# Top-k attention and a SoLU block on one core: from priorities to a fixed order of four engines

## The chip, the cores and the metric

The kernel runs on one core of a Trainium2 chip. The core has five engines that run side by side and meet through semaphores: PE (TensorE, matrix products and transposes; PEld is its weight load), ACT (ScalarE), DVE (VectorE), POOL (GpSimd) and SP (SyncE, which here issues the DMAs). Each takes its instructions in the order in which they stand in its program. The metric is device time in microseconds (us), less is better. Before the change it is 1582.19 us, the median of three runs (1580.61 to 1582.75).

## The reference

For each of 8 batches and 8 heads there are 576 queries, keys and values of 64 elements, in float32.

```
scores = q @ k.T / 8                              # 576 x 576 per head
kth    = the 32nd largest score of each row
P      = softmax(scores where scores >= kth, else -1e9)
attn   = P @ v                                    # 576 x 64 per head
x      = attn as 4608 tokens x 512                # the 8 heads side by side
h      = x @ w_in                                 # 512 -> 1024
solu   = h * softmax(h)
ln     = (solu - mean) / sqrt(var + 1e-6) * g_ln  # over the 1024
out    = ln @ w_out                               # 1024 -> 512
```

The weights arrive as float64, so the kernel first turns their words into float32 on DVE and POOL.

## The kernel before

**Work.** `fast_path` handles two heads of a batch at a time: 32 pairs. The 576 rows of two heads are 9 row tiles of 128 (four per head, and the two tails of 64 together). A general path follows in the program for inputs on which the search below fails; it is not taken here.

**One pair, in order of its data.** `load_qk` (SP) loads q and k. `prep_t`, `prep_m` (PE) transpose them, `prep_tc`, `prep_mc` (ACT) copy them out of PSUM. `moments` (PE) multiplies k with itself, `moments_c` (ACT) copies the result, `spread` (PE) multiplies it with q, `spread_v` and `spread_r` (DVE) reduce that to a spread per row, `first_p` (POOL, a power) and `first` (DVE) make a first threshold `t0` of it. `scores` (PE) makes the rows, `evac` (ACT) copies each row tile to SBUF as X. `count0` (DVE, `junkv`, L760) counts the scores over `t0`, nine instructions; `second` (DVE, its last at L775) makes `t1`; `count1` (ACT, `junka`, L783) counts again, nine instructions; `third` (DVE, L792 to L800) makes `t2`; `count2` (ACT, `sg`, L815) counts a third time. `side`, `nearest` (DVE, `al` L824 and `w` L836, L840) take the eight scores next to `t2`, `kth` (DVE) picks the 32nd. `exps` (ACT, E, L847), `keep` (DVE, L877), `inverse` (DVE) and `norm` (POOL, L892) make P; `transpose_p`, `transpose_last` (PE) and `copy_p`, `copy_last` (ACT) turn it; `attn_v` (PE) multiplies it with v, and `copy_v` (ACT, `xTm`, `xTt`) leaves x.

**One token tile.** 128 tokens, 36 in all: four per batch, and one of tails per two batches. `mm1` (PE, `h_ps`, L976), `hmax` (DVE), `hexp` (ACT), `solu` (DVE), `square` (ACT), `ln` (POOL, L1016 to L1021), `transpose_ln` (PE), `copy_ln` (ACT), `mm2` (PE, `o_ps`, L1040), `store` (ACT, then a DMA). A batch has four pairs, so a tile goes with each pair, and every eighth pair has one more.

**What sets the order.** Every step is put into a list with a time (`at`), the list is sorted, and the steps are traced in that order. The times are formulas, `STEP` = 38 apart from pair to pair, a token tile's from its own number. That trace is only a priority. Behind it a scheduler with a cost model of its own orders the instructions of each engine, and may take a later one first.

**Buffers.** PSUM has three pools of two buffers each: `ps_big` (two banks each: scores, `h_ps`, `y_ps`), `ps_tp` (one bank: all transposes and, before, `moments`) and `ps_o` (one bank: `om`, `ot`, `o_ps` and `y_t`). qm and km have one buffer each, X six, E three, `w_raw` two.

**Weights.** `load_w` (SP) loads a chunk of 128 x 512 float64, 16 chunks; `weights_step` runs a part of its conversion. Before, the first step of a chunk also issues the load of the next one.

Of the kernel before, what the change touches and what calls it, by code (L numbers as in the profile page):

```python
# [15 lines left out]
P = 128  # L16
# [427 lines left out]
def fast_path(  # L444
# [129 lines left out]
    xs = {}  # L574

# [27 lines left out]

    def prep_t(i):

        d = st[i]
        d["qkT"] = p2.tile([P, 2, S], F32, tag="qkT", name="qkT")
        tp = d["tp_t"] = ps_tp.tile([P, NM, P], F32, tag="tp", name="tp_t")
        for n, nm in enumerate("qk"):
            nc.tensor.transpose(  # L610
                tp[:, 0, n * ST : (n + 1) * ST], d[nm + "t"].rearrange("p h d -> p (h d)"),
                ident[0:ST, 0:ST],
            )

# [39 lines left out]
    def moments_c(i):  # L654
        d = st[i]
        nc.scalar.copy(out=d["mom"][:, 0:D], in_=d["tm"][:, 0:D])

    def spread(i):
# [4 lines left out]
        d["yt"] = ps_o.tile([P, 512], F32, tag="o", name="y_t")[:, 0 : D + 1]  # L663
# [93 lines left out]
    def count0(i, j):  # L757
# [4 lines left out]
            op0=ALU.is_ge, op1=ALU.add, accum_out=d["c0"][:, j : j + 1],  # L762
        )

    def second(i):
# [11 lines left out]
        d["n1"] = small.tile([P, NT], F32, tag="n1", name="n1")  # L777
        d["n2"] = small.tile([P, NT], F32, tag="n2", name="n2")

    def count1(i, j):  # L780
# [4 lines left out]
            bias=d["t1"][:, j : j + 1], accum_out=d["n1"][:, j : j + 1],  # L785
        )

    def third(i):
# [16 lines left out]
        d["al"] = small.tile([P, NT], F32, tag="al", name="al")  # L805
        d["w8"] = small.tile([P, NT, 8], F32, tag="w8", name="w8")
# [5 lines left out]
    def count2(i, j):  # L812
# [4 lines left out]
            bias=d["t2"][:, j : j + 1], accum_out=d["n2"][:, j : j + 1],  # L817
        )

    def side(i, g):  # L820
# [4 lines left out]
            out=d["al"][:, js], in0=d["n2"][:, js], scalar=512.5, in1=d["tt"][:, js],  # L825
# [3 lines left out]
    def nearest(i, j):  # L829
# [10 lines left out]
        nc.vector.max(d["w8"][:, j, :], w)  # L840

    def exps(i, g):
        d = st[i]
        if g == 0:
            d["E"] = [None] * NG
        d["E"][g] = p3.tile([P, 3, S], F32, tag="E", name="E")
        nc.scalar.activation(out=d["E"][g], in_=d["X"][g], func=AF.Exp)  # L847

    def kth(i):
# [13 lines left out]
        nc.vector.tensor_tensor(out=hot, in0=hot, in1=d["w8"], op=ALU.mult)  # L863
# [8 lines left out]
        d["rden"] = small.tile([P, NT], F32, tag="rden", name="rden")  # L872
# [24 lines left out]
    def p_of(i, j):  # L897
        return st[i]["E"][j // 3][:, j % 3, :]
# [5 lines left out]

    def copy_p(i, j):
        d = st[i]
        if j == 0:
            d["PT"] = [None, None]
        if j % 4 == 0 and j < 2 * NM:
            d["PT"][j // 4] = p2.tile([P, 2, NM + 1, 2 * P], F32, tag="PT", name="PT")  # L910
        if j < 2 * NM:
            t, h = divmod(j, 2)
            dst = d["PT"][t // 2][:, h, 0:NM, t % 2 * P : (t % 2 + 1) * P]
        else:
            d["PTt"] = p1.tile([P, NM + 1, P], F32, tag="PTt", name="PTt")
            dst = d["PTt"][:, 0:NM, :]
# [8 lines left out]
    def copy_last(i, part):  # L925
        d = st[i]
        tp = d.pop(("tpl", part))
        if part == 2:
            nc.scalar.copy(out=d["PTt"][0:ST, NM, :], in_=tp[0:ST, 0, :])
            return  # L930
        dst = d["PT"][part][0:ST, :, NM, :].rearrange("p h (t s) -> p t h s", t=2)
        nc.scalar.copy(out=dst, in_=tp[0:ST].rearrange("p (t h) s -> p t h s", h=2))

    def attn_v(i, part):
        b, hp = pairs[i]
        d = st[i]
        if part == 0:
            if hp == 0:
                xs["m", b] = p2.tile([P, NP, SM], F32, tag="xTm", name="xTm")
                if b % 2 == 0:  # L940
                    xs["t", b // 2] = p2.tile([P, NP, 2 * ST], F32, tag="xTt", name="xTt")
            d["om"] = ps_o.tile([P, 512], F32, tag="o", name="om")
        elif part == 2:
            d["ot"] = ps_o.tile([P, 512], F32, tag="o", name="ot")
        vm, vt = d["v"]
        o = d["ot"][:, 0:ST] if part == 2 else d["om"][:, part * 2 * P : (part + 1) * 2 * P]

        for c in range(NM + 1):
# [22 lines left out]
    def mm1(d):  # L971
        x = d["x"]()
        h = ps_big.tile([P, 2, 512], F32, tag="big", name="h_ps")
        for half in range(2):
            for c in range(NP):
                nc.tensor.matmul(  # L976
                    out=h[:, half, :], lhsT=x[:, c, :],
                    rhs=w_in[:, c, half * 512 : (half + 1) * 512],
                    start=(c == 0), stop=(c == NP - 1),
                )  # L980
        d["h"] = h.rearrange("p a f -> p (a f)")

    def hmax(d):
        d["nmax"] = small.tile([P, 1], F32, tag="hmax", name="hmax")
        nc.vector.tensor_reduce(out=d["nmax"], in_=d["h"], axis=AX.X, op=ALU.max, negate=True)  # L985

    def hexp(d):
# [3 lines left out]
            out=d["e"], in_=d["h"], func=AF.Exp, bias=d["nmax"], accum_out=d["rs"]  # L991
        )

    def solu(d):
# [6 lines left out]
            out=d["solu"], in0=d["h"], scalar=rs, in1=d["e"], op0=ALU.mult, op1=ALU.mult,  # L1001
# [30 lines left out]
    def copy_ln(d, g):  # L1032
        if g == 0:
            d["lnT"] = p2.tile([P, NF, P], F32, tag="lnT", name="lnT")
        nc.scalar.copy(out=d["lnT"][:, 4 * g : 4 * g + 4, :], in_=d["tp", g])  # L1035

    def mm2(d):
        d["o"] = ps_o.tile([P, 512], F32, tag="o", name="o_ps")
        for c in range(NF):
            nc.tensor.matmul(  # L1040
                out=d["o"], lhsT=d["lnT"][:, c, :], rhs=w_out[:, c, :],
# [12 lines left out]
    STEP = 38.0  # L1054
# [4 lines left out]
    def pair_times(i):  # L1059
        b = i * STEP  # L1060
        at(b - 32, load_qk, i)
        at(b + 1, load_v, i)

        at(b - 17.2, prep_t, i)
        at(b - 17.1, prep_m, i, "q")
        at(b - 16.8, prep_tc, i)
        at(b - 16.5, prep_mc, i, "q")
        at(b - 16.4, prep_m, i, "k")
        at(b - 15.4, prep_mc, i, "k")
        at(b - 15.3, moments, i)  # L1070
        at(b - 14.6, moments_c, i)
        at(b - 14.2, spread, i)
        at(b - 13.2, spread_v, i)
        at(b - 12.4, spread_r, i)
        at(b - 12.0, first_p, i)
        at(b - 6.5, first, i)

        for t in range(NM + 1):
            at(b - 9.6 + 1.6 * t, scores, i, t)
        for j in range(NT):  # L1080
            at(b - 8.4 + 0.8 * j, evac, i, j)
            at(b - 3.5 + 0.77 * j, count0, i, j)
            at(b + 5.0 + 0.77 * j, count1, i, j)
            at(b + 16.0 + 0.77 * j + (2.5 if j > 4 else 0), count2, i, j)
        at(b + 4.0, second, i)
        at(b + 12.6, third, i)

        b += STEP
        for g, t in enumerate((12.0, 14.4, 19.5)):
            at(b + t, exps, i, g)  # L1090
            at(b + 4.9 + 4.26 * g, side, i, g)
            at(b + 28.0 + 2.3 * g, inverse, i, g)
        at(b + 22.6, kth, i)
        for j in range(NT):
            at(b + 5.0 + 1.42 * j, nearest, i, j)
            at(b + 25.5 + 0.75 * j, keep, i, j)
            at(b + 29.0 + 0.9 * j, norm, i, j)
            at(b + 30.4 + 0.9 * j, transpose_p, i, j)
            at(b + 30.9 + 0.9 * j, copy_p, i, j)
        for part, t in enumerate((33.6, 37.2, 38.0)):  # L1100
            at(b + t, transpose_last, i, part)
            at(b + t + 0.6, copy_last, i, part)
# [115 lines left out]
```

## Time and profile before

| | before |
|---|---|
| median of three runs | 1582.19 us |
| the profiled execution | 1580.09 us, span of its instructions 1578.2 us |
| busy in the span: PE, DVE, ACT, POOL | 84%, 74%, 72%, 32% |
| PE weight loads busy | 48% |
| HBM traffic over the span | 30 GB/s |

The span has three stretches. I mark them by the first `count1` instruction of a pair (L783): the first pair's is at 43.5 us, the ninth's at 404.08, the last pair's at 1410.97. Up to 404 us the weights are converted beside the first pairs, from there every pair takes the same 43 us (a little more where a tile of tails comes in), and after 1411 us the last pair and the last token tiles run out. A busy share is an average over these. Matmuls are pipelined and the ends of their records are modelled, so PE's busy time is more than PE needs.

### The profile page before, as it was taken

To read this page: it belongs to the slowest core of one execution; us is meant where nothing else is said; L and a number is where in the kernel's file an instruction comes from. 1 tells how busy PE (TensorE), PEld (TensorE's weight loads), DVE (VectorE), ACT (ScalarE), POOL (GpSimd) and SP (SyncE) were. 2 spreads that over 40 slices of the span, in tenths; PEclk is the share of its full clock that TensorE was granted. 3 is DMA by queue.
4 is the path that set the end of the run, shared out by engine and by line. 5 is a ranking of instruction groups with operands and counts; after the bars stand their busy time and mean duration, and the time that the engine had idled before them with its cause. 6 is when DMAs were issued, how large, how long until landed. Compare 5 with 4: busy or idle time off the path is not lost.

```text
span 1578.2 us, 21450 instructions
## 1 busy us (share of the span) xinstructions
PE 1332.5 (84%) x7043; PEld 751.8 (48%) x7043; DVE 1168.7 (74%) x2976; ACT 1144.2 (72%) x2398; POOL 505.4 (32%) x613
## 2 busy tenths in 40 slices
PE   5461576679989899998898899998989889998997
PEld 3231344445545555555554455555555445554543
DVE  4685878887778888877777788877777778877111
ACT  3574557788878877878887887877888778876322
POOL 5667452222222222222222222312222222323110
PEclk9565766688999999999999999998999999999999
DMA  4211101111110001111111100111011110000000
GB/s 109 69 35 56 56 15 24 24 24 31 31 31 24 23 24 30 31 34 26 31 31 31 31 22 17 31 37 31 24 31 31 31 31 16 23 22 7 14 21 22
DMA packets 101898, 48.67 MB, mean 31 GB/s; under 512 B 86921, under 2 KB 95121, under 8 KB 101777
## 3 DMA queue, kind: packets, MB, share of 16 engines
q1 hardware_dynamic: 101776, 47.21, 11.1%
q8 instruction: 57, 0.93, 0.2%
q14 instruction: 65, 0.52, 0.1%
HBM read 37.75 MB, written 9.44 MB: 30 GB/s over the span
## 4 chain that ended last, share of the span: by engine, by line
DVE 36%; PE 27%; ACT 19%; POOL 11%; issue 6%; DMA 0%; SPq 0%; ACTq 0%; POOLq 0%; DVEq 0%
ACT junka L783 9%; DVE w L836 9%; DVE junkv L760 8%; DVE w L840 8%; PE o_ps L1040 7%; PE h_ps L976 6%; ACT sg L815 4%; PE s_ps L741 4%; POOL zs L706 3%; PE om L952 3%; PE tp_ln L1028 2%; PE tp_p L903 2%; DVE E L877 2%; POOL E L892 2%; POOL w_tmp L43 2%
## 5 line engine op out<-in xcount | busy, mean ns | idle before, releaser
L892 POOL TENSOR_SCALAR E<-E,rden 128x576 f32<-128x576 f32 x288 | 227.4, 805 | 746.9 <-ACT xTt L964 424.3
L741 PE MATMUL s_ps<-qkT 64*128 64x288 f32 (+1 forms) x1280 | 284.5, 504 | 66.2 <-ACT X L752 29.9
L783 ACT ACTIVATE junka<-X,t 128x576 bf16<-128x576 f32 x288 | 220.1, 767 | 107.6 <-DVE t L775 104.5
L752 ACT ACTIVATE X<-s_ps 128x576 f32<-128x576 f32 x288 | 175.1, 649 | 135.3 <-PE s_ps L741 131.3
L1040 PE MATMUL o_ps<-w_out,lnT 128*128 128x512 f32 x576 | 253.1, 593 | 0.6 <-ACT lnT L1035 0.5
L877 DVE SCALAR_TENSOR_TENSOR E<-X,kth,E 128x576 f32<-128x576 f32 x288 | 228.4, 826 | 10.6 <-ACT E L847 6.9
L815 ACT ACTIVATE sg<-X,t 128x576 bf16<-128x576 f32 x288 | 220.0, 767 | 21.9 <-DVE t L800 20.6
L976 PE MATMUL h_ps<-w_in,xTm 128*128 128x512 f32 x512 | 231.0, 601 | 0.0
L836 DVE SCALAR_TENSOR_TENSOR w<-X,al,sg 128x576 f32<-128x576 f32 x288 | 228.1, 811 | 0.0
L741 PEld LDWEIGHTS s_ps<-qkT 64*128 64x128 f32 (+1 forms) x1280 | 160.5, 213 | 139.2 <-ACT X L752 53.5
L760 DVE TENSOR_SCALAR_CACHE_REDUCE junkv<-X,t 128x576 bf16<-128x576 f32 x288 | 222.6, 805 | 0.5 <-ACT X L752 0.5
L840 DVE MAX8 w<-w 128x8 f32<-128x576 f32 x288 | 213.2, 752 | 0.0
L903 PE MATMUL tp_p<-ident,E 128*128 128x128 f32 x1152 | 183.4, 293 | 16.6 <-POOL E L892 13.7
L903 PEld LDWEIGHTS tp_p<-ident,E 128*128 128x128 f32 x1152 | 130.9, 147 | 101.7 <-issue 46.6
L917 ACT COPY PT<-tp_p 128x512 f32<-128x512 f32 x256 | 145.2, 593 | 46.5 <-PE tp_p L903 46.4
L1040 PEld LDWEIGHTS o_ps<-w_out,lnT 128*128 128x128 f32 x576 | 109.2, 190 | 138.7 <-issue 132.5
L847 ACT ACTIVATE E<-X 128x1728 f32<-128x1728 f32 x96 | 158.0, 1646 | 0.7 <-PE tp_pt L923 0.6
L952 PE MATMUL om<-PT,vm 128*64 128x256 f32 x1024 | 146.4, 387 | 0.0
L976 PEld LDWEIGHTS h_ps<-w_in,xTm 128*128 128x128 f32 x512 | 95.0, 191 | 106.8 <-issue 105.2
L627 PE MATMUL tp_qk<-ident,km 128*128 128x128 f32 x128 | 29.6, 372 | 110.7 <-ACT qkT L617 110.7
L824 DVE SCALAR_TENSOR_TENSOR al<-n,tt 128x3 f32<-128x3 f32 x96 | 27.6, 288 | 107.2 <-ACT sg L815 105.8
L985 DVE TENSOR_REDUCE hmax<-h_ps 128x1 f32<-128x1024 f32 x36 | 43.7, 1214 | 72.8 <-PE h_ps L976 72.8
(114 smaller groups left out, 1628.8 us busy)
## 6 DMA issues: line engine op xcount, KB each, us to landing
qm<-in_q_dram SPq DMA_DIRECT2D x32, 256.0 KB, 3.4
km<-in_k_dram SPq DMA_DIRECT2D x32, 256.0 KB, 3.4
vm<-in_v_dram SPq DMA_DIRECT2D x32, 256.0 KB, 2.8
out_dram<-osb SPq DMA_DIRECT2D x32, 256.0 KB, 2.3
w_raw<-in_moe_w_in_dram SPq DMA_DIRECT2D x8, 512.0 KB, 3.8
w_raw<-in_moe_w_out_dram SPq DMA_DIRECT2D x8, 512.0 KB, 3.5
qt<-in_q_dram SPq DMA_DIRECT2D x32, 32.0 KB, 2.2
kt<-in_k_dram SPq DMA_DIRECT2D x32, 32.0 KB, 2.8
```

Source lines behind the costliest of these rows:

```text
L741: nc.tensor.matmul(out=s[:, half, 0:SH], lhsT=qkT[hd, 0, qs], rhs=qkT[hd, 1, half * SH : (half + 1) * SH], start=True, stop=True,)
L760: nc.vector.tensor_scalar(out=junk, in0=x_of(i, j), scalar1=d["t0"][:, j : j + 1], scalar2=None, op0=ALU.is_ge, op1=ALU.add, accum_out=d[" ...
L783: nc.scalar.activation(out=junk, in_=x_of(i, j), func=AF.Sign, scale=-1.0, bias=d["t1"][:, j : j + 1], accum_out=d["n1"][:, j : j + 1],)
L815: nc.scalar.activation(out=d["sg", j], in_=x_of(i, j), func=AF.Sign, scale=-(1.0 + 2.0**-23), bias=d["t2"][:, j : j + 1], accum_out=d["n2" ...
L836: nc.vector.scalar_tensor_tensor(out=w, in0=x_of(i, j), scalar=d["al"][:, j : j + 1], in1=d.pop(("sg", j)), op0=ALU.subtract, op1=ALU.mult,)
L840: nc.vector.max(d["w8"][:, j, :], w)
L877: nc.vector.scalar_tensor_tensor(out=e, in0=x_of(i, j), scalar=d["kth"][:, j : j + 1], in1=e, op0=ALU.is_ge, op1=ALU.mult, accum_out=den_a ...
L892: nc.gpsimd.tensor_scalar(out=e, in0=e, scalar1=st[i]["rden"][:, j : j + 1], scalar2=1.0, op0=ALU.mult, op1=ALU.mult,)
L903: nc.tensor.transpose(tp[:, c, :], p_of(i, j)[:, c * P : (c + 1) * P], ident)
L952: nc.tensor.matmul(out=o[h * D : (h + 1) * D, :], lhsT=vm[:, h, c, :] if c < NM else vt[:, h, :], rhs=rhs[0:ks, c, :], start=(c == 0), sto ...
L976: nc.tensor.matmul(out=h[:, half, :], lhsT=x[:, c, :], rhs=w_in[:, c, half * 512 : (half + 1) * 512], start=(c == 0), stop=(c == NP - 1),)
L1040: nc.tensor.matmul(out=d["o"], lhsT=d["lnT"][:, c, :], rhs=w_out[:, c, :], start=(c == 0), stop=(c == NF - 1),)
```

## The change

It does five things. (1) The four engines PE, ACT, DVE and POOL run in the order of the trace itself: the trace is put under `manual_schedule`, and no scheduler moves their instructions. SP is not among the four. (2) The order comes from tables: for each step of a pair and of a token tile the place relative to the pair's start, for each of its instructions by itself (nine numbers for the nine `count0`). `STEP` is 39. There are three tables for token tiles (ordinary, tails, the last batch), and lists for the weights. (3) `mm1` and `mm2` are two halves that can stand apart. (4) The transposes of the tails of q and k, `moments`, and the last rows of `spread` share one tile `pre` in `ps_o`, in place of two buffers of `ps_tp` and one of `ps_o`. (5) `load_w` has times of its own. Helpers (`once`, `columns`) make a tile at its first use, whichever step comes first; they issue nothing. `d.clear()` at a pair's end is gone, which is bookkeeping of the trace alone.

```diff
@@ finish_w
-        if n + 1 < len(w_chunks):
-            load_w(n + 1)
...
+    def pre_of(i):
+        return once(st[i], "pre", lambda: ps_o.tile([P, 512], F32, tag="o", name="pre"))
@@ prep_t
-        tp = d["tp_t"] = ps_tp.tile([P, NM, P], F32, tag="tp", name="tp_t")
+        pre = pre_of(i)
@@ moments
-        tm = d["tm"] = ps_tp.tile([P, NM * P], F32, tag="tp", name="tp_m")
+        tm = d["tm"] = pre_of(i)[:, 2 * ST : 2 * ST + D]
@@ spread
-        d["yt"] = ps_o.tile([P, 512], F32, tag="o", name="y_t")[:, 0 : D + 1]
+        d["yt"] = d["pre"][:, 4 * D : 5 * D + 1]
...
-    def mm1(d):
+    def mm1(d, half):
         x = d["x"]()
-        h = ps_big.tile([P, 2, 512], F32, tag="big", name="h_ps")
-        for half in range(2):
-            for c in range(NP):
...
+        h = once(d, "h", lambda: ps_big.tile([P, 2, 512], F32, tag="big", name="h_ps"))
+        for c in range(NP):
...
-    def mm2(d):
-        d["o"] = ps_o.tile([P, 512], F32, tag="o", name="o_ps")
-        for c in range(NF):
+    def mm2(d, half):
+        o = once(d, "o", lambda: ps_o.tile([P, 512], F32, tag="o", name="o_ps"))
+        for c in range(half * NM, (half + 1) * NM):
...
-    STEP = 38.0
+    STEP = 39
...
+        (count0, range(9), [1.62, 0.66, 0.53, -0.25, 1.6, 0.92, 1.48, 3.07, 3.12]),
+        (mm1, range(2), [50.27, 49.14]),
...
+    with tc.manual_schedule(engines={E.PE, E.Activation, E.DVE, E.Pool}):
+        for _, _, f, args in sorted(todo, key=lambda x: x[:2]):
+            f(*args)
```

Three places show what moved. The line numbers in the order of the changed kernel are its own.

DVE before, in the middle of the program: from the first threshold (the first row is the first half of `first`) to the ninth `count0` and the start of `second` (`r`). `junkv` is `count0`, `w` is `nearest`.

```order
L716 TENSOR_TENSOR t_7332<-mean,zs 128x9
L836 SCALAR_TENSOR_TENSOR w<-X,al,sg 128x576
L718 SCALAR_TENSOR_TENSOR ta<-zs,t_7332 128x9
L760 TENSOR_SCALAR junkv,c_7293<-X,t_7332 128x576 x2
L840 MAX w_7144<-w 128x8
L760 TENSOR_SCALAR junkv,c_7293<-X,t_7332 128x576 x2
L836 SCALAR_TENSOR_TENSOR w<-X,al,sg 128x576 x2
...
L760 TENSOR_SCALAR junkv,c_7293<-X,t_7332 128x576
L840 MAX w_7144<-w 128x8
L768 TENSOR_SCALAR r<-c_7293 128x9
```

DVE now, the same steps of a later pair, up to the end of `second`.

```order
L732 TENSOR_TENSOR t_7871<-mean,zs 128x9
L734 SCALAR_TENSOR_TENSOR ta<-zs,t_7871 128x9
L772 TENSOR_SCALAR junkv,c_7883<-X,t_7871 128x576 x3
L844 SCALAR_TENSOR_TENSOR w<-X,al,sg 128x576
L849 MAX w_7740<-w 128x8
L772 TENSOR_SCALAR junkv,c_7883<-X,t_7871 128x576 x6
L780 TENSOR_SCALAR r<-c_7883 128x9
L783 RECIPROCAL r<-r 128x9
L785 TENSOR_TENSOR u<-r,tb 128x9
L787 TENSOR_TENSOR t_7922<-u,ta 128x9
```

Before, the nine `count0` of a pair stand among all nine `nearest` of the pair ahead; now one `nearest` is left among them, four go ahead of `first` and four follow `second`.

PE before, from the weighted values of a pair (`om`, `ot`) to the first scores: the token tile's `h_ps` and `o_ps` in one piece, then the preparation of the next pair, with the token tile's transposes (`tp_ln`) among it (the 20 rows of moments and the 20 of spread are left out).

```order
L952 MATMUL ot<-PTt,vt 64x64 x2
L976 MATMUL h_ps<-w_in,xTm 128x512 x8
L1040 MATMUL o_ps<-w_out,lnT 128x512 x8
L610 MATMUL tp_t<-ident,qt 128x64
L610 MATMUL tp_t<-ident,kt 128x64
L627 MATMUL tp_qk<-ident,qm 128x128 x4
L627 MATMUL tp_qk<-ident,km 128x128 x4
...
L1028 MATMUL tp_ln<-ident,solu 128x128 x4
...
L668 MATMUL y_t<-mom,qkT 64x65
L1028 MATMUL tp_ln<-ident,solu 128x128 x4
L741 MATMUL s_ps<-qkT 128x288 x4
```

PE now, the same stretch.

```order
L644 MATMUL tp_qk<-ident,qm 128x128 x4
L960 MATMUL om<-PT,vm 64x256 x8
...
L934 MATMUL tp_pt<-ident,E 64x128
L986 MATMUL h_ps<-w_in,xTm 128x512 x8
...
L644 MATMUL tp_qk<-ident,km 128x128 x4
L627 MATMUL pre<-ident,qt 128x64
L627 MATMUL pre<-ident,kt 128x64
L1051 MATMUL o_ps<-w_out,lnT 128x512 x4
...
L684 MATMUL pre<-mom,qkT 64x65
L909 MATMUL tp_p<-ident,E 128x128 x8
L1051 MATMUL o_ps<-w_out,lnT 128x512 x4
L755 MATMUL s_ps<-qkT 128x288 x4
```

The transposes of q stand before `h_ps`, those of k, the tails and the moments right behind it, half of `o_ps` before the spread and half behind it, and no `tp_ln` stands ahead of the spread.

ACT before, from a pair's last `count1` to its `evac` rows (X), and ACT now.

```order
L783 ACTIVATE junka,n_8322<-X,t_8320 128x576 x3
L847 ACTIVATE E<-X 128x1728
L990 ACTIVATE e_sb,rs<-h_ps,hmax 128x1024
L815 ACTIVATE sg,n_8323<-X,t_8387 128x576 x5
L1010 ACTIVATE e_sb,var<-solu,nmu 128x1024
L1047 COPY osb<-o_ps 128x512
L617 COPY qkT<-tp_t 128x2x64
L635 COPY qkT<-tp_qk 128x512
...
L1035 COPY lnT<-tp_ln 128x512 x2
L752 ACTIVATE X<-s_ps 128x576 x4
```

```order
L793 ACTIVATE junka,n_8793<-X,t_8770 128x576 x3
L854 ACTIVATE E<-X 128x1728
L976 COPY xTt<-ot 128x64
L1002 ACTIVATE e_sb,rs<-h_ps,hmax 128x1024
L672 COPY mom<-pre 128x64
L655 ACTIVATE qkT,mom<-tp_qk 128x512
L634 COPY qkT<-pre 128x2x64
L823 ACTIVATE sg,n_8898<-X,t_8885 128x576 x4
...
L764 ACTIVATE X<-s_ps 128x576 x2
L928 COPY PT<-tp_p 128x4x128
```

The three copies of the preparation stand before the first `count2` (`sg`) now; before, five `count2`, `square` and `store` stood ahead of them. On SP the first two loads are weight chunks now, ahead of the first q; before, q and k came first.

## Rows read from the trace of the kernel before

**Rows 1.** Busy time by stretch; columns: stretch, its length, then each engine.

```profile
core 0: us, PE busy (x) PEld busy (x) DVE busy (x) ACT busy (x) POOL busy (x), PEclk, DMA share, GB/s
43.47:404.08 360.61, 222.91 (x1316) 135.85 (x1316) 285.93 (x701) 242.89 (x523) 166.27 (x158) 0.70 0.13 36
...
404.08:1410.97 1006.89, 932.04 (x5070) 525.26 (x5069) 808.26 (x2090) 818.16 (x1724) 278.82 (x377) 0.94 0.11 28
...
1060.92:1410.97 350.05, 323.63 (x1762) 182.47 (x1761) 280.86 (x727) 284.46 (x600) 96.69 (x131) 0.94 0.10 27
1410.97:1478.50 67.53, 59.38 (x296) 32.42 (x295) 38.10 (x101) 42.01 (x84) 21.22 (x25) 0.95 0.02 9
1478.50:1578.20 99.70, 91.23 (x248) 42.26 (x246) 18.23 (x38) 24.72 (x43) 11.59 (x18) 0.98 0.06 20
```

**Rows 2.** The same view for the instructions of `count1` (L783) alone.

```profile
43.47:404.08 360.61, 56.77 (x145) 0.70 0.13 36
404.08:1410.97 1006.89, 165.15 (x415) 0.94 0.11 28
```

**Rows 3.** Waits of ACT from 1060.92 to 1410.97: total us, times, longest.

```profile
ACT junka L783 <- DVE t L775: 32.5, 9, 4.4
ACT X L752 <- PE s_ps L741: 20.8, 30, 1.6
ACT PT L917 <- PE tp_p L903: 9.0, 8, 1.2
ACT e_sb L990 <- DVE hmax L985: 5.4, 8, 1.0
```

**Rows 4.** Chain of waits from 840 to 884 us: start, length, what.

```profile
840.23 3.90 ACT junka L783 x10
...
857.37 1.20 POOL solu L1021
...
862.86 1.82 POOL zs L706
...
874.25 1.46 DVE junkv L760 x4
...
877.25 0.66 DVE w L840
877.91 1.45 DVE w L836 x2
...
883.27 0.77 ACT junka L783
```

**Rows 5.** One stretch of a period: busy time, granted clock in the third column from the end.

```profile
856.70:861.20 4.50, 4.05 (x32) 2.79 (x32) 1.66 (x6) 4.50 (x13) 1.73 (x2) 0.53 0.45 125
```

**Rows 6.** Chain of waits at the end.

```profile
1477.35 0.88 PE ot L952 x20
...
1487.86 6.87 PE h_ps L976 x16
...
1570.62 0.58 ACT osb L1047
```

**Rows 7.** Groups of instructions by shape: count, busy us, mean ns, idle before.

```profile
L1040 PE MATMUL o_ps<-w_out,lnT 128*128 128x512 f32 x576 | 253.1, 593 | 0.6 <-ACT lnT L1035 0.5
...
L847 ACT ACTIVATE E<-X 128x1728 f32<-128x1728 f32 x96 | 158.0, 1646 | 0.7 <-PE tp_pt L923 0.6
...
L985 DVE TENSOR_REDUCE hmax<-h_ps 128x1 f32<-128x1024 f32 x36 | 43.7, 1214 | 72.8 <-PE h_ps L976 72.8
...
L990 ACT ACTIVATE e_sb<-h_ps,hmax 128x1024 f32<-128x1024 f32 x36 | 40.2, 1116 | 29.6 <-DVE hmax L985 27.4 <-DVE rden L885 2.1
...
L617 ACT COPY qkT<-tp_t 128x128 f32<-128x128 f32 x32 | 8.3, 260 | 5.0 <-PE tp_t L610 5.0
...
L656 ACT COPY mom<-tp_m 128x64 f32<-128x64 f32 x32 | 6.4, 201 | 0.0
```

**Rows 8.** DMA issues: size of one, median us from issue to landing.

```profile
w_raw<-in_moe_w_in_dram SPq DMA_DIRECT2D x8, 512.0 KB, 3.8
```

More of the change, by code (lines that the diff above doesn't have):

```diff
@@ L574, in fast_path, with once, columns @@
     xs = {}
+    def once(d, key, make):
+        if key not in d:
+            d[key] = make()
+        return d[key]
+    def columns(i, tag, n=NT):
+        return once(st[i], tag, lambda: small.tile([P, n], F32, tag=tag, name=tag))
     def load_qk(i):
@@ L1053, in fast_path @@
     todo = []
-    STEP = 38.0
+    STEP = 39
     def at(time, f, *args):
         todo.append((time, len(todo), f, args))
[L1059 to L1102, printed above, removed]
-        for part, t in enumerate((36.0, 38.4, 40.4)):
-            at(b + t, attn_v, i, part)
-        at(b + STEP + 8.1, copy_v, i, 1)
-        at(b + STEP + 8.9, copy_v, i, 2)
@@ L1108, in token_times @@
-    def token_times(n, x, stores, more=0.0):
-        d = {"x": x, "stores": stores}
-        late = n > NPAIR + 1
-        b = (NPAIR + 1) * STEP + 10.0 + 15.0 * (n - NPAIR - 2) if late else n * STEP + more
-        at(b + 5.5, mm1, d)
-        at(b + 12.8, hmax, d)
-        at(b + 14.2, hexp, d)
-        at(b + 16.5, solu, d)
-        at(b + 20.0, square, d)
-        at(b + 21.5, ln, d)
-        lt, c = (27.7, 29.0) if late else (25.5, STEP + 12.7 - more / 2)
-        for g in range(2):
-            at(b + lt + 0.3 * g, transpose_ln, d, g)
-            at(b + lt + 0.6 + 0.4 * g, copy_ln, d, g)
-        at(b + c, mm2, d)
-        at(b + c + 7.3, store, d)
@@ new lines, in fast_path @@
+    token_times = [
+        (mm1, range(2), [50.27, 49.14]),
+        (hmax, [()], [54.98]),
+        (hexp, [()], [55.64]),
+        (solu, [()], [59.22]),
+        (square, [()], [61.34]),
+        (ln, [()], [61.97]),
+        (transpose_ln, range(2), [66.04, 69.62]),
+        (copy_ln, range(2), [68.1, 70.94]),
+        (mm2, range(2), [96, 100.9]),
+        (store, [()], [111.09]),
+    ]
+    tails_times = [
+        (mm1, range(2), [49.3, 58.2]),
+        (hmax, [()], [59.66]),
+        (hexp, [()], [62.71]),
+        (solu, [()], [62.9]),
+        (square, [()], [65.35]),
+        (ln, [()], [84.81]),
+        (transpose_ln, range(2), [96.98, 101]),
+        (copy_ln, range(2), [100.23, 104.48]),
+        (mm2, range(2), [104.33, 115]),
+        (store, [()], [118.99]),
+    ]
@@ new lines, in fast_path @@
+    last_times = [
+        (mm1, range(2), [71.33, 69.92]),
+        (hmax, [()], [78.16]),
+        (hexp, [()], [78.81]),
+        (solu, [()], [83.04]),
+        (square, [()], [83.59]),
+        (ln, [()], [100.44]),
+        (transpose_ln, range(2), [102.58, 110.88]),
+        (copy_ln, range(2), [112.49, 115.16]),
+        (mm2, range(2), [115.09, 125.08]),
+        (store, [()], [136.53]),
+    ]
+    load_w_times = [
+        -112.27, -234.02, -23.8, 43.75, 86.36, 115.75, 158.47, 141.69, 9.29, 24.95, 97.57,
+        119.83, 148.55, 196.44, 208.35, 238.25,
+    ]
@@ new lines, in fast_path, with all_times @@
+    weights_times = [
[5 rows of a table added]
+    ]
+    at(-25.26, load_g)
+    for n in range(len(w_chunks)):
+        at(load_w_times[n], load_w, n)
+        for time in weights_times[3 * n : 3 * n + 3]:
+            at(time, weights_step, n)
+    def all_times(base, table, *first):
+        for f, args, times in table:
+            for a, time in zip(args, times):
+                at(base + time, f, *first, *(() if a == () else (a,)))
+    for i in range(NPAIR):
+        all_times(i * STEP, pair_times, i)
+    for b in range(B):
```

206 lines of the change are left out of this document (116 added, 90 removed), and 5 rows, old and new, of the table weights_times.

## The prediction

> **What bounds the kernel now.** I began with the busy time by stretch. From 404.08 to 1410.97 us there are 415 records of `count1`, 18 a pair (nine instructions and their nine accumulator reads), so 23 pairs in 1006.89 us, 43.78 each [rows 1, 2]. Before that 8 pairs take 360.61, 45.1 each, and 167.2 us follow (67.5 until the last pair's weighted values are out, then 99.7). The reader is to see that in the long middle no engine is full. A cycle of eight pairs with its nine token tiles, 1060.92 to 1410.97, is 350.05 long; a pair's share of it is 43.76, of which ACT is busy 284.46/8 = 35.56, DVE 280.86/8 = 35.11, POOL 12.1 [rows 1]. So ACT stands idle 8.2 us a pair. The view of waits says for what: 32.5 us in the eight pairs for `t1` before `count1`, 20.8 for scores, 9.0 for transposes, 5.4 for `hmax` [rows 3].
>
> The chain of waits of one period shows why `t1` is late. It runs from `count1` (840.23) through the token tile's work to POOL's normalisation at 857.37, its transposes on PE, the spread, the power on POOL at 862.86, then `count0` with `nearest` in turns on DVE (874.25 to 877.91), to `count1` again at 883.27 [rows 4]. It is a ring of 43.04 us: the token tile stands in it because its transposes are ahead of the spread on PE, and 18 `nearest` instructions stand in it because they share the stretch with `count0`. DMA does not appear in it.
>
> **The change, part by part.** *The ring.* Nothing is computed less; instructions move. On DVE nine `count0` (0.73 each, from 1.46 for two and their reads) now have one `nearest` (0.72 + 0.66) among them, not nine [rows 4]. On PE the spread no longer has the token tile's transposes ahead, and on ACT its copies are ahead of `count2`. So the two pieces that made `t1` late leave the ring. What is late next? The new ring through `count1`: beside it, between `second` and `third`, DVE has four `nearest` (4 x 1.38), three `keep` and `hmax` (1.21), together 8.9 us if a `keep` is as long as a `count0`, and `kth` [rows 4, 7]; `count1` and the two copies in it are 11 instructions of at most 0.78 (3.90 for five and reads [rows 4]), 8.6 us. They lie beside each other, so this ring is not longer than DVE's own work. The bound is then the fuller engine, ACT with 35.56, plus the waits that stay.
>
> Which stay: the waits for `t1` and `hmax` go (37.9 us in eight pairs), the ones for scores and transposes I keep whole, 29.8/8 = 3.7, since PE still feeds ACT through the same two buffers each. That makes 39.3 a pair. The ends: 36.1 if all but half a microsecond goes, and 43.8 if each wait that goes comes back in a fixed queue, where an engine can't take a later instruction meanwhile; I take 39.3 as it is the measured list less two of its rows. Middle: 23 x (43.78 - 39.3) = 103 us.
>
> *PE.* Its busy time per pair, 323.63/8 = 40.45, is above that, but records overlap: one 512-column matmul lasts 593 ns in the profile [rows 7], while sixteen of them take 6.87 us, 429 ns each [rows 6]. A token tile is 2 x 6.87, with 9/8 tiles a pair 15.5 us; the other 25 us of busy time shrink, by the same 429/593, to 18. So 33.5, between the weight loads' 182.47/8 = 22.8 below and 40.45 above [rows 1]. It fits under 39.3.
> The Trainium skill says so too (Trace Analysis, Identifying the Most-Contended Engine): matmul busy share does not measure how near PE is to its limit, the weight loads' share does. Its rule would put PE at 52% here, and taken the other way, by the busy share, PE would be the bound; that is the first rival.
>
> *The halves* of `mm1` and `mm2` issue the same instructions; that they stand apart costs nothing on PE and lets 3.43 us (half of 6.87) cover the copies on ACT before the spread. *The shared bank.* Moments, tails and the last spread rows use one buffer, so the spread's writes wait for both copies, 0.20 and 0.26 us [rows 7]. The spread reads the first anyway; new is at most 0.26 a pair, 8 us over 32, if ACT is late. Between tails and spread stands half an `mm2`, 3.43 us, which hides 0.46; I take 0. Gone the other way: two of 18 uses of `ps_tp` a pair.
> A rule of the Trainium skill speaks against it (Trace Analysis, Optimizing Tensor Performance, Matmuls): independent groups should go through different PSUM banks, so that the evacuation of one lies beside the next one's matmuls. By the rule PE would stand still 0.26 to 0.46 a pair; the sum would be 8 to 15 us worse. No row of before shows a shared bank.
>
> *Waits that are added.* ACT now stands at the copies of moments, k and tails before the first `count2`; queued behind are all `count2`, and DVE's `side` waits for those. PE reaches these steps after `h_ps`. While it does, ACT has nine `count1`, E (1.65) and `hexp` (1.12) [rows 7]. I price it at 0 and keep it as a rival. *SP* issues the same loads; a 512 KB load lands in 3.8 us [rows 8], and q and k are half of that each; their buffers come free at the spread's products on DVE, most of a period ahead of the next transposes of q, so I price that queue at 0 in the middle. The first q, however, stands behind two weight chunks now: 0 to 7.6 us, I take 5.
>
> *First pairs.* DVE is busy 285.93/8 = 35.7 a pair, POOL 20.8, ACT 30.4, and PE runs at a granted 0.70 [rows 1]. The floor is about 36; it took 45.1. I take 41, half of what lies above the floor, since conversion on POOL and PE's low clock stay; the ends are 37 and 45.1. A batch's tiles also start one pair earlier. 8 x 4.1 = 33, less 5 for the start: 28.
>
> *The end.* After the last weighted values (1477.35) PE is busy 91.23 of 99.7 us with token tiles [rows 1, 6]. One tile, 13.7 us, is now done earlier. The gain lies between 0 and 13.7, as the first tile's chain has nothing else beside it; I take 8. The rest, the last copy at 1570.62 and the store, stays.
>
> **Sum.** 103 + 28 + 8 = 139 us off 1580.09, the profiled execution: 1441. The median of the runs is 2.1 above that execution, so 1443.
>
> **Rivals.**
> 1. PE's busy time is real work: a pair then costs 40.45 and some hand-over, 41. For it: in most of a period PE shows busy throughout. Against: 593 against 429 ns. Middle 64, first pairs 28, end 0: 1580 - 92 + 2 = 1490.
> 2. Slower: `h_ps` late. PE takes `h_ps` only after the last transpose of the pair ahead; `hmax` and `hexp` follow, and ACT queues all `count2` behind `hexp`. From ACT's last P copy, PE needs 6.87 and DVE 1.2, about 9 with the transpose; ACT has some 10 of work (nine `count1`, E, copies). At half clock `h_ps` takes 13.7, ACT waits 5.6 more and a pair costs 44.9. PE did run at a granted 0.53 of its clock, its lower level of 1.2 GHz, in a stretch after it had waited [rows 5]. Against: `h_ps` comes right behind dense work, and shows 6.87. Then the middle loses 26, the first pairs gain nothing and the start loses 5, the end gains 8: 1605. With no gain in the first pairs it decides from 4.6 us a pair over 39.3.
> 3. Half of it comes back on DVE: `first` stands in a fixed place and waits for POOL's power, which has six `norm` and the token's normalisation ahead. If it is 3 us late, a pair costs 42.3. For it: the power is in the chain today [rows 4]. Against: POOL has 12.1 us of work a pair, and DVE has four `nearest` before `first`. Middle 34, first pairs 10, end 8: 1530.
> 4. The waits for PE go as well, 36.1 a pair, the first pairs at 38, the end 13.7: 177 + 52 + 14 off: 1340.
>
> **How the numbers follow.** Forecast 0.58, with 37.6 to 40.6 us a pair and the ends of the other two terms about 1380 to 1500; rival 1 0.16, rival 2 0.08, rival 3 0.10, rival 4 0.08. The time is the forecast's, 1443. The range 1390 to 1530 holds nearly all of the forecast and rival 1, and half of rival 3, about 0.8. No change means within 0.2%, some 3 us, which is what a measurement of this kernel can tell. Faster 0.90, same 0.02 (the far edge of rival 3), slower 0.08.
>
> **What would show it.** Right: `count1` of neighbouring pairs about 39 us apart; waits of ACT for `t1` and `hmax` nearly gone, those for scores and transposes about as now; ACT and DVE busy nine tenths of a period; the spread no longer in the chain. Rival 1 would show PE without idle at 41, rival 2 ACT waiting for `hmax` or the copies behind it and a low clock, rival 3 DVE waiting for the power. I am wrong if a pair costs over 41, or if the first pairs don't come under 43.

## The result, and the profile after

The changed kernel takes 1422.72 us (median of 4 runs, 1422.27 to 1423.23), the kernel before 1582.21 on the same chip (4 runs): a ratio of 0.8994, interval 0.8978 to 0.9009. The forecast was 1443, so 20 us were missing from a sum of 139. Stage by stage the two traces differ like this: first `count1` at 29.20 instead of 43.47 us (14.3 gained; I had priced a loss of 5), eight first pairs in 324.3 instead of 360.6 (36.3 gained, I had 33), 23 pairs of the middle in 916.9 instead of 1006.9 (90.0 gained, I had 103), the rest in 150.7 instead of 167.2 (16.5 gained, I had 8). These are the rows that answer to [rows 1, 2]: busy time by stretch of the changed kernel, with the columns as there; the third stretch is one ordinary pair, the fourth a cycle of eight, the fifth the three pairs of that kind of cycle beside the tile of tails, and the last two are the end.

```profile
core 0: us, PE busy (x) PEld busy (x) DVE busy (x) ACT busy (x) POOL busy (x), PEclk, DMA share, GB/s
29.20:353.52 324.32, 237.18 (x1367) 139.24 (x1367) 310.47 (x708) 252.26 (x538) 192.60 (x168) 0.77 0.16 44
353.52:1270.42 916.90, 875.62 (x5060) 482.86 (x5060) 867.44 (x2089) 805.71 (x1722) 327.36 (x377) 0.98 0.12 31
...
951.09:989.80 38.71, 36.72 (x219) 20.33 (x218) 37.42 (x91) 34.39 (x75) 14.04 (x16) 1.00 0.12 32
632.78:951.09 318.31, 304.22 (x1762) 167.99 (x1761) 301.58 (x727) 280.29 (x600) 113.83 (x131) 0.98 0.12 32
826.52:951.09 124.57, 121.58 (x685) 67.00 (x684) 114.45 (x277) 107.79 (x230) 43.60 (x51) 0.99 0.12 32
1270.42:1333.47 63.05, 55.70 (x310) 30.44 (x308) 49.09 (x113) 41.75 (x84) 21.50 (x25) 0.97 0.04 14
1333.47:1421.10 87.63, 80.24 (x218) 37.32 (x218) 15.23 (x32) 20.75 (x37) 9.69 (x15) 0.97 0.06 19
```

Two things are to be seen. The middle is not one kind of pair: five of eight take 38.7 us, and the three beside the tile of tails take 124.57 together, 8.4 more than three ordinary ones. And DVE, which does the same instructions as before, is busy 301.58/8 = 37.7 us a pair, not 35.1 [rows 1]; in an ordinary pair that is 97% of the time. ACT's share is 35.0, from 35.56.

The waits of ACT in that cycle answer to [rows 3] (total us, times, longest):

```profile
ACT e_sb L1002 <- DVE hmax L997: 13.5, 8, 2.2
ACT junka L793 <- DVE t L787: 10.9, 8, 2.0
ACT X L764 <- PE s_ps L755: 5.5, 8, 1.4
```

The wait for `t1` fell from 32.5 to 10.9 and its longest from 4.4 to 2.0. The wait for scores, which I kept, fell from 20.8 to 5.5, and that for `hmax`, which I took out, grew from 5.4 to 13.5. ACT waits for DVE. The chain of waits of the ordinary pair, which answers to [rows 4], says the same; here are pieces of it, in order of time (start, length, what):

```profile
954.98 0.76 DVE w L849
955.74 0.73 DVE w L844
956.49 0.76 DVE w L849
...
958.85 2.31 DVE E L883 x6
961.16 1.14 DVE hmax L997
...
973.49 0.61 DVE rden L891
974.12 0.18 DVE rden L894
974.30 0.51 DVE al L832
...
977.98 1.12 DVE w L844
979.13 0.76 DVE w L849
979.89 0.57 DVE t L732
...
980.65 2.19 DVE junkv L772 x6
```

L844 and L849 are the two instructions of `nearest`, L883 is `keep`, L772 `count0`. Nearly every piece is on DVE: the ring through the token tile and the spread is gone, as forecast, and a full engine stands in its place; not the one I named. Four rows are odd: 0.61 us for a `rden` and 0.51 for an `al` of three columns each, 1.12 for a `w` that takes 0.73 some rows above, 0.57 for a `t` of nine columns. The timelines of DVE and POOL in that stretch show what they have in common (start, length, engine and line):

```profile
973.49 0.60 DVE L891 TENSOR_SCALAR rden<-den_all 128x3 f32<-128x3 f32 x1
974.12 0.18 DVE L894 RECIPROCAL rden<-rden 128x3 f32<-128x3 f32 x1
974.22 0.58 DVE L832 SCALAR_TENSOR_TENSOR al<-n,tt 128x3 f32<-128x3 f32 x1
...
977.90 1.20 DVE L844 SCALAR_TENSOR_TENSOR w<-X,al,sg 128x576 f32<-128x576 f32 x1
979.13 0.76 DVE L849 MAX8 w<-w 128x8 f32<-128x576 f32 x1
979.81 0.64 DVE L732 TENSOR_TENSOR t<-mean,zs 128x9 f32<-128x9 f32 x1
```

```profile
971.61 3.18 POOL L898 TENSOR_SCALAR E<-E,rden 128x576 f32<-128x576 f32 x3
974.87 0.21 POOL L718 TENSOR_SCALAR zs<-ss 128x9 f32<-128x9 f32 x1
975.16 2.18 POOL L722 TENSOR_TENSOR zs<-zs,phalf 128x9 f32<-128x9 f32 x1
977.44 0.21 POOL L724 TENSOR_SCALAR tb<-zs 128x9 f32<-128x9 f32 x1
977.74 2.69 POOL L898 TENSOR_SCALAR E<-E,rden 128x576 f32<-128x576 f32 x3
```

Each slow instruction lies beside three `norm` of POOL (L898). The means by line over the middle show it for `w` (`nearest`) and `E` (`keep`). First the kernel before, 404.08 to 1410.97 us:

```profile
L836 DVE SCALAR_TENSOR_TENSOR w<-X,al,sg 128x576 f32<-128x576 f32 x207 | 161.9, 803 | 0.0
L877 DVE SCALAR_TENSOR_TENSOR E<-X,kth,E 128x576 f32<-128x576 f32 x207 | 160.5, 809 | 2.6
L760 DVE TENSOR_SCALAR_CACHE_REDUCE junkv<-X,t 128x576 bf16<-128x576 f32 x207 | 159.9, 806 | 0.0
```

Then the changed kernel, 353.52 to 1270.42 us:

```profile
L844 DVE SCALAR_TENSOR_TENSOR w<-X,al,sg 128x576 f32<-128x576 f32 x208 | 177.8, 855 | 1.6
L883 DVE SCALAR_TENSOR_TENSOR E<-X,kth,E 128x576 f32<-128x576 f32 x207 | 173.8, 872 | 2.6
...
L772 DVE TENSOR_SCALAR_CACHE_REDUCE junkv<-X,t 128x576 bf16<-128x576 f32 x207 | 155.1, 806 | 0.4
```

The one-input `count0` is 806 ns in both. Over the whole run of the changed kernel `w` and `E` have means of 866 and 895, and POOL's `norm`, whose fast ones take about 750, has 959:

```profile
L898 POOL TENSOR_SCALAR E<-E,rden 128x576 f32<-128x576 f32 x288 | 272.3, 959 | 30.7 <-DVE rden L894 22.6
```

The Trainium skill has a rule for this (GPSIMD Engine Reference, Key points): GpSimd shares its SBUF interfaces with VectorE and contends with VectorE instructions that run in a 2-port mode or have two SBUF inputs. The trace agrees for `w` and `E`: with no POOL work beside them they take 809 and 814 ns on average, with POOL busy throughout 961 and 1073, while MAX stays at 761. The prediction had not used it. In which mode `rden`, which has one input, ran, no trace here shows. The small instructions are not new, though: in the middle of the kernel before `al` and `rden` had means of 292 and 309 ns, in the changed kernel 274 and 294.

At the end, answering to [rows 6], the chain is token products back to back, in pieces of 3.43 us:

```profile
1340.53 20.60 PE h_ps L986 x48
1361.13 0.87 PE tp_ln L1040 x8
1362.01 3.44 PE h_ps L986 x8
1365.44 3.43 PE o_ps L1051 x8
...
1413.67 0.59 ACT osb L1058
```

### The profile page after: what moved, and what is told of

Same layout as the page of the kernel before. It is cut to its first block, busy times and chain, and to the rows that moved or that the text cites. A ratio compares the mean times of both kernels' runs of the same rounds, so it can differ in the third digit from the quotient of the medians.

```text
span 1421.1 us, 21446 instructions
## 1 busy us (share of the span) xinstructions
PE 1268.8 (89%) x7043; PEld 701.9 (49%) x7043; DVE 1255.7 (88%) x2976; ACT 1129.8 (80%) x2398; POOL 567.4 (40%) x613
## 4 chain that ended last, share of the span: by engine, by line
DVE 54%; PE 29%; ACT 8%; issue 6%; POOL 1%; DMA 1%; SPq 0%; DVEq 0%; ACTq 0%; POOLq 0%
DVE w L844 11%; DVE E L883 10%; DVE w L849 10%; DVE junkv L772 9%; PE h_ps L986 8%; PE o_ps L1051 8%; PE s_ps L755 4%; ACT junka L793 4%; PE tp_p L909 3%; PE om L960 3%; DVE solu L1012 2%; DVE hmax L997 2%; DVE rden L891 1%; ACT sg L823 1%; PE tp_ln L1040 1%
## 5 line engine op out<-in xcount | busy, mean ns | idle before, releaser
L898 POOL TENSOR_SCALAR E<-E,rden 128x576 f32<-128x576 f32 x288 | 272.3, 959 | 30.7 <-DVE rden L894 22.6
L1051 PE MATMUL o_ps<-w_out,lnT 128*128 128x512 f32 x576 | 269.3, 612 | 16.4 <-ACT xTt L976 16.4
L986 PE MATMUL h_ps<-w_in,xTm 128*128 128x512 f32 x512 | 238.2, 617 | 19.3 <-ACT xTm L971 19.3
L844 DVE SCALAR_TENSOR_TENSOR w<-X,al,sg 128x576 f32<-128x576 f32 x288 | 249.5, 866 | 2.2
L883 DVE SCALAR_TENSOR_TENSOR E<-X,kth,E 128x576 f32<-128x576 f32 x288 | 248.2, 895 | 3.4
L755 PE MATMUL s_ps<-qkT 64*128 64x288 f32 (+1 forms) x1280 | 247.3, 466 | 4.3 <-ACT X L764 2.2
L816 POOL TENSOR_SCALAR tt<-t 128x9 f32<-128x9 f32 x32 | 6.7, 211 | 572.9 <-DVE rden L891 572.3
L849 DVE MAX8 w<-w 128x8 f32<-128x576 f32 x288 | 219.2, 761 | 9.9
L772 DVE TENSOR_SCALAR_CACHE_REDUCE junkv<-X,t 128x576 bf16<-128x576 f32 x288 | 216.1, 806 | 2.7 <-ACT X L764 2.3
L755 PEld LDWEIGHTS s_ps<-qkT 64*128 64x128 f32 (+1 forms) x1280 | 134.5, 191 | 82.9 <-ACT X L764 25.3
L960 PE MATMUL om<-PT,vm 128*64 128x256 f32 x1024 | 126.3, 389 | 0.0
L1002 ACT ACTIVATE e_sb<-h_ps,hmax 128x1024 f32<-128x1024 f32 x36 | 40.2, 1115 | 73.9 <-DVE hmax L997 67.7
```

The lines of the kernel that those rows point to most:

```text
L755: nc.tensor.matmul(out=s[:, half, 0:SH], lhsT=qkT[hd, 0, qs], rhs=qkT[hd, 1, half * SH : (half + 1) * SH], start=True, stop=True,)
L772: nc.vector.tensor_scalar(out=junk, in0=x_of(i, j), scalar1=d["t0"][:, j : j + 1], scalar2=None, op0=ALU.is_ge, op1=ALU.add, accum_out=col ...
L844: nc.vector.scalar_tensor_tensor(out=w, in0=x_of(i, j), scalar=d["al"][:, j : j + 1], in1=d.pop(("sg", j)), op0=ALU.subtract, op1=ALU.mult,)
L849: nc.vector.max(w8[:, j, :], w)
L883: nc.vector.scalar_tensor_tensor(out=e, in0=x_of(i, j), scalar=d["kth"][:, j : j + 1], in1=e, op0=ALU.is_ge, op1=ALU.mult, accum_out=den_a ...
L898: nc.gpsimd.tensor_scalar(out=e, in0=e, scalar1=st[i]["rden"][:, j : j + 1], scalar2=1.0, op0=ALU.mult, op1=ALU.mult,)
```

## The experiments

**Is the gain in the table or in the fixing?** The changed kernel without the fixed order:

```
-    with tc.manual_schedule(engines={E.PE, E.Activation, E.DVE, E.Pool}):
-        for _, _, f, args in sorted(todo, key=lambda x: x[:2]):
+    for _, _, f, args in sorted(todo, key=lambda x: x[:2]):
```

> The new table is kept as priorities, but the order on the four engines is left to the scheduler, which works with its own durations. Theory (the places in the table are the gain, whoever issues them): 1425 to 1450 us. Rival (the gain is that the order is fixed, since the scheduler's durations put work elsewhere than the table says): 1500 to 1580 us, with ScalarE waiting for the first count again (30 us or more in eight pairs).

And the kernel before with its own due times, wrapped in that same line.

> The kernel before with its old due times, but with the order fixed by them on the four engines. Theory (the measured places are the gain): the old due times, fixed, are no better than what the scheduler made of them: 1580 us or more. Rival (fixing the order is the gain): about 1450 us.

Measured: 1565.21 us (ratio 0.9896, 0.9854 to 0.9939) and 1859.85 us (1.1759, 1.156 to 1.1959). The theory of the first fell: all that was changed without the fixed order gains 16 us of 159. So did the rival of the second: fixing the old order loses 278. In the first, ACT's wait for `t1` is back (eight pairs):

```profile
ACT junka L793 <- DVE t L787: 36.7, 6, 8.8
```

In the second, DVE's `count0` waits for scores 43 times in 400 us, some seven and a half pairs, and PE ran at a mean granted clock of 0.806 over the run:

```profile
DVE junkv L760 <- ACT X L752: 55.7, 43, 3.7
DVE yq L686 <- PE y_ps L668: 39.0, 7, 8.5
```

The gain needs both: an order that fits the durations, and that it is kept.

**Which engine is full?** One more count on DVE a pair, behind `kth`; then one more pass of 576 columns on ACT.

```
...
+        nc.vector.tensor_scalar(
+            out=junk, in0=x_of(i, 0), scalar1=1.0, scalar2=None, op0=ALU.mult, op1=ALU.add,
+            accum_out=hot[:, 0, 0:1],
+        )
```

> The changed kernel with one more DVE instruction a pair, a count over 576 scores behind kth, whose result nobody reads. Theory A, DVE is the bound of a pair (busy 37.4 of 38.7 us): 0.73 to 0.8 us more in each pair, some 23 to 26 us in all, about 1447 us. Theory B, ACT with its waits is the bound, as predicted: DVE has 1.3 us idle a pair and takes it in, 1423 to 1428 us.

```
+        if g == 1:
...
+            nc.scalar.activation(out=junk, in_=x_of(i, 0), func=AF.Copy)
```

> The changed kernel with one more ACT instruction a pair, a copy of 576 scores behind the second exponential (about 0.65 us), whose result nobody reads. Theory A (DVE bounds): ACT is busy 34.4 of 38.7 us and takes it in, 1423 to 1427 us. Theory B (ACT bounds): 0.65 more a pair, about 1443 us.

Measured: 1435.71 us (1434.48 to 1436.94) and 1423.28 (1423.21 to 1423.35). A DVE instruction of about 0.8 us makes an ordinary pair 0.44 us longer (39.15 against 38.71), one on ACT nothing (38.69). So ACT does not set the period, against my prediction. DVE nearly does: 13 us lie between the 23 to 26 of theory A and the 5 at most of theory B, so neither range was met.

**What does POOL cost DVE?** `norm` scales 8 of the 576 columns only; the rest of the probabilities stay unscaled.

```
-        e = p_of(i, j)
+        e = p_of(i, j)[:, 0:8]
```

> The normalisation of P on POOL runs over 8 of the 576 columns; the others stay unnormalised, so the output is not the reference's. DVE's orders and instructions are those of the changed kernel. Theory A1, DVE's two-input instructions (w from 811 to 866 ns, E from 826 to 895 ns) are longer because POOL works beside them: their means go back to about 810 and 815, some 1.2 us a pair, 37.5 a pair, about 1387 us. Theory A2, they are longer for another reason (ACT, PE or DMA on the same data): means stay at 866 and 895 and the time within some 5 us of 1423, as the normalisation is not in the chain.

Measured: 1364.36 us (1363.78 to 1364.94), 58 us less, more than expected; 37.8 of them lie in the middle, 17.7 in the first pairs. Yet POOL had only 1% of the changed kernel's chain. The ordinary pairs of a cycle take 35.6 to 36.6 us, 36.0 on average, 2.7 less. DVE gives back 2.4 of that, by the starts of its instructions: `keep` 0.63, `w` 0.42, and the small `al`, `rden` and `t` 0.44, 0.43 and 0.49; MAX gives nothing. The small ones I had not counted on. Busy time of the pair of 35.61, and of the three pairs of its cycle beside the tails:

```profile
641.09:676.70 35.61, 35.54 (x218) 19.86 (x217) 34.36 (x90) 34.44 (x76) 9.72 (x16) 1.00 0.13 34
```

```profile
785.54:910.53 124.99, 122.50 (x688) 67.38 (x687) 110.96 (x280) 107.68 (x230) 30.41 (x51) 0.99 0.12 31
```

Those three did not get shorter (124.99 against 124.57), with PE busy 98% and some three quarters of their chain on PE. In the changed kernel the chain of those three is mixed, 46% PE, 33% DVE and 18% ACT. So DVE sets the ordinary pairs, and PE those three, as far as the relief of DVE shows it; no run gave PE itself more or less work.

**Dependent instructions back to back.** `nearest` split in two steps, so that one `w` or count stands between a `w` and its MAX; places of the second step:

```
...
+        (
+            largest, range(9),
+            [39.925, 28.035, 32.5, 31.72, 48.27, 32.2, 50.59, 50.295, 50.585],
+        ),
```

> The same work as the changed kernel; each nearest is two steps with places of their own (its product w, and the largest eight of w), and another DVE instruction stands between the two: w4, side, w7, max4, w8, max7, w6, max8, max6 and so on. Theory A3, a DVE instruction right behind the one that it reads costs more (w and max back to back 1.51 us in the changed kernel, 1.39 in turns before): about 0.12 to 0.15 for 9 of them, 1.1 to 1.3 us a pair, about 1385 to 1390 us. If DVE does not bound, or the order of the two costs nothing: 1423 us.

Measured: 1408.52 us (1406.96 to 1409.5), ratio 0.8901 (0.8887 to 0.8916). The direction holds, the size is about half: the ordinary pair is 38.09, not 38.71. From start to start, `w` and MAX together went from 14.1 to 13.0 us a pair, but 0.4 of that is a `w` that no longer lies beside `norm` (1.23 us in the changed kernel), so some 0.7 is left for the turns. `E` and `ta`, now elsewhere against POOL's work, took back 0.3 and 0.5. Of the kernels that leave nothing out it is the fastest here.

**Norms to ACT.** In that kernel, norms 6 to 8 of each pair on ACT:

```
+        if j >= 6:
+            nc.scalar.activation(
+                out=e, in_=e, func=AF.Copy, scale=st[i]["rden"][:, j : j + 1]
+            )
+            return
```

> The kernel with nearest and largest in turns, and in it three of the nine norms of each pair taken from GpSimd and given to ScalarE. Theory (VectorE sets the period, and GpSimd beside it stretches its instructions; ScalarE has room): a third of what the small norm gave, 0.6 to 0.9 us a pair, 1380 to 1390 us against 1408.5. Rival (ScalarE, 34.4 us busy a pair and 2 us more, becomes the bound, or a norm in its queue holds up the counts): 1408 us or more.

Then the same with `if j >= 6 and i % 8 in (7, 0, 1, 2)`:

> The kernel with turns, and three of nine norms on ScalarE only in pairs 0, 1, 2 and 7 of every eight, whose norms fall into pairs without the tile of tails. Theory (VectorE sets the ordinary pair, where three norms off GpSimd were worth 0.65 us; in the two pairs beside the tails ScalarE and TensorE set it, and there the norms on ScalarE cost 4 to 5 us an eight): about 0.65 us in half of the pairs and no loss beside the tails, 1396 to 1402 us against 1408.5. Rival (what ScalarE gets is given back in the next pairs anyway): 1406 to 1415 us.

Measured: 1414.31 us (1412.8 to 1420.72) and 1414.18 (1409.1 to 1416.71). Both miss; in both the rival held, and neither is faster than the kernel with turns. The ordinary pair did fall by 0.65, as expected, to 37.44. In the first the pairs beside the tails grew (three of them 126.5 to 129.8 us, against 124.1 to 125.5 in the kernel with turns; read from an execution of 1420.72 us); in the second most pairs next to those that gained took 0.2 to 3.3 us more, and what ACT was given came back there. The cycle of the first:

```profile
631.19:949.15 317.96, 305.36 (x1762) 168.71 (x1762) 291.78 (x727) 295.15 (x624) 94.00 (x107) 0.99 0.12 32
```

DVE lost 6 us of busy time in eight pairs against the kernel with turns (297.81), ACT gained 15. The chain of its whole run is 39% PE, 36% ACT and 21% DVE.

**The halves and the bank.** The token products whole again:

```
-        (mm2, range(2), [96, 100.9]),
+        (mm2, range(2), [96, 96.001]),
```

(and so for `mm1` and the other two tables).

> The changed kernel with the token products whole again (the two halves of the first adjacent, the halves of the second adjacent). Theory (VectorE sets the period and the spread products have slack on TensorE): at most 0.5 us a pair, 1423 to 1440 us. Rival (the whole product ahead of the spread lands on the chain, up to 2 us a pair on TensorE and back): about 1.7 to 3.4 us a pair, 1480 to 1500 us.

The old PSUM banks in the fixed order:

```
-        tm = d["tm"] = pre_of(i)[:, 2 * ST : 2 * ST + D]
+        tm = d["tm"] = ps_tp.tile([P, NM * P], F32, tag="tp", name="tp_m")[:, 0:D]
```

(and so for tails, and `y_t` in the output's pool).

> The changed kernel with the old PSUM banks: tails and moments in the bank pool of the transposes, y_t in that of the outputs; the order stays fixed. Theory (the shared bank neither costs nor gives): 1418 to 1428 us. Rival (a matmul behind one to another bank is quicker, so more banks gain): 1408 to 1415 us. Second rival (the transposes wait for the moments' bank): over 1435 us.

Measured: 1452.61 us (two runs, 1452.59 and 1452.62) and 1459.17 (1457.6 and 1460.74). Joined costs 30 us, 1.2 a pair in the middle (41.05 against 39.87), between theory and rival. Both halves of the second product now stand ahead of the spread; both behind it was not tried. Its waits in eight pairs show where (us, times, longest):

```profile
DVE yq L702 <- PE y_ps L684: 17.8, 8, 3.2
```

The spread comes 2 us later in each pair, and DVE, full as it is, stands still for it. With the old banks 36 us are lost, 1.4 a pair in the middle. The second rival held:

```profile
ACT X L764 <- PE s_ps L755: 18.8, 8, 3.2
...
PE tp_t L627 <- ACT mom L672: 15.9, 8, 3.5
```

In each pair PE stands before the tails' transposes until ACT has copied the moments, about 2 us, and the scores are late behind it. The places are those that were made for the shared bank; a table made for the old banks was not tried. In the changed kernel neither this wait nor that of DVE for `y_ps` is in the list.

**The start.** The six steps of the first two weight chunks all ahead of the first spread; the loads as in the change.

```
-        -6.25, -3.69, 16.93, -56.15, -25.57, -7.52, 8.09, 9.97, 66.68, 82.54, 90, 94.35, 102.87,
+        -60.5, -60.4, -60.3, -60.8, -60.7, -60.6, 8.09, 9.97, 66.68, 82.54, 90, 94.35, 102.87,
```

> The changed kernel with the six steps of the first two weight chunks all ahead of the first spread on VectorE and GpSimd, the loads in the order of the change. Theory (what set the start of the kernel before is that the first pair's spread and its powers stood behind the weight steps): the first count moves from 29.2 to 35 to 37 us, and the total to 1420 to 1430 us, since the steps moved are gone from later places. Rival (the start is set by the loads and TensorE): the first count stays at 29 to 31 us.

Measured: first `count1` at 37.6 us (0.6 above the range given), in all 1430.33 (1430.04 to 1430.62), 0.3 above its range. The whole 8 us stay to the end. POOL in the start of this kernel:

```profile
18.75 1.26 POOL L50 TENSOR_TENSOR w_tmp<-w_tmp 128x512 f32<-128x512 f32 x1
22.42 0.21 POOL L718 TENSOR_SCALAR zs<-ss 128x9 f32<-128x9 f32 x1 [2.41 <-DVE ss L713]
22.71 1.84 POOL L722 TENSOR_TENSOR zs<-zs,phalf 128x9 f32<-128x9 f32 x1
```

In the changed kernel that power starts at 14.73, ahead of the second chunk's steps.

## Why the prediction was right or wrong

*The sum.* 1443 against 1422.72 is nearer than its parts: the middle gave 13 us less than forecast, the start, the first pairs and the end 31 more. That they cancel in part is luck.

*What goes.* Right: the token tile's transposes, the spread's matmuls and the power left the ring through `t1`; none of them is in the chain of the ordinary pair. Eight of the nine `nearest` left the stretch of `count0`. They are still in the chain, with 38% of it, but as part of DVE's own work.

*What bounds it next.* Wrong, and this is the step that failed: "The bound is then the fuller engine, ACT with 35.56, plus the waits that stay." I took DVE's 35.1 as a constant. It became 37.7 for the same instructions. About 1.0 of the 2.6 is that POOL now works beside `w` and `E` (nine times 52 and nine times 63 ns a pair), and some 0.7 that `w` and its MAX now follow each other directly, by the kernel with turns. The rest was not taken apart; the small ones add nothing in all, since `al` and `rden` were as slow before. ACT has room. The waits for scores and transposes, kept at 3.7 us a pair, shrank too (that for scores from 20.8 to 5.5 in eight pairs), so an ordinary pair came out at 38.7 against 39.3: near for a wrong reason. The 39.87 of the mean is this and the three pairs that PE sets. Two errors of opposite sign hid each other.

*PE.* "It fits under 39.3" holds for five pairs of eight (with `norm` cut they take 35.6 to 36.6), not for the other three, which have an extra tile and take 41.7 a pair even with DVE relieved. Rival 1 is right there and only there. The weight loads are busy 67.38/124.99 = 54% in that very stretch, the matmuls 98%. So the rule of the Trainium skill that the prediction followed (Trace Analysis, Identifying the Most-Contended Engine) misled here. The matmul share alone tells no more: with `norm` cut it is 35.54 of 35.61 us in the ordinary pair too, and the chain of that pair is DVE's.

*Halves and bank, priced at 0.* Wrong as parts: taken back one by one they cost 30 and 36 us. The forecast named the cover (copies on ACT before the spread) but gave it no price, since it had DVE with room. With the old banks the tails' transposes wait for the moments' copy, 15.9 us in eight pairs. The rule of the Trainium skill that spoke against the shared bank (Trace Analysis, Optimizing Tensor Performance, Matmuls) did not decide here: with these places, the old banks are the slower ones.

*First pairs.* Right in number, 40.5 us each against 41, not in reason. I took DVE's 35.7 as the floor and half of what lay above it. DVE was busy 310.47 of 324.32 us in this stretch, 38.8 a pair, with POOL at 192.60: full, not waiting. The first two of the eight took 28.3 and 38.1 us, the last 38.7, the five between 42.6 to 44.3.

*The start.* Wrong sign: I counted the weights ahead of the first q on SP (a loss of 5) and did not see that on DVE and POOL the first spread and power moved ahead of the weights' steps. Putting the weights' steps back ahead of the spread costs 8 of the 14.3 us; where the rest comes from was not tried.

*The end.* Right in kind, too small: 12.1 us in the last stretch, near my bound of 13.7, and 4.5 in the one ahead of it, which I had left out.

*Rivals.* Rival 2 (PE late, half clock) did not come: PEclk is 1.00 in the ordinary pair. Rival 3 did not come: DVE waited for no power in the eight pairs. Rival 4 came in part: the waits for PE went, but DVE took their room.

## What to carry to other kernels

When an order is fixed, ask of the fullest engine not only how long its instructions took but what ran beside them: POOL work that has next to no part in the chain can still lengthen the period through VectorE. Treat busy time as a property of the order, and test it by one cheap instruction added on each engine that might be the bound. A table of places and its fixing are one change: here the one without the other gave a tenth of the gain, or a loss. Pieces that look free (halves, a bank) can be worth what the full engine would wait without them.

## What the runs showed of the hardware that was not expected

A `norm` of 128x8 instead of 128x576 on POOL brought VectorE's `w` and `E` in the middle from 855 and 872 to 820 and 818 ns, and its `t` of 128x9 from a mean of 689 to 152. Beside `norm`, the small `al` and `rden` took up to 0.6 us and `t` up to 1.0, instead of 0.15 to 0.17. Single `w` and `E`, most of which take 0.81 us, took up to 1.23 and 1.29 in the middle; the longest of the run, 1.9 and 1.8, lay beside the weight conversion (L50) in the first pairs. `count0` and MAX took 806 and 761 ns, with POOL work beside them or not. Nine `w` and MAX one behind the other took 14.1 us from start to start, with one instruction between them 13.0; some 0.7 of the difference is the order, 0.4 the place of one `w` against POOL.
